# A linear-attention kernel with a squared-relu layer behind it: four paired squares split, and the five engines' lists reordered

## The chip, the cores and the metric

The kernel runs on one core of one Trainium2 chip. The metric is the device time of one execution in microseconds (us). In the profile PE is TensorE (matmuls), PEld its weight loads, DVE VectorE, ACT ScalarE, POOL GpSimd and SP SyncE, which here only issues transfers. L1051 is line 1051 of the kernel's file.

## What is computed

A gated linear attention over 768 tokens for 4 batches of 8 heads with 48 channels, and behind it, token by token, a two-layer network with a squared relu:

```
for t in range(S):
    state = alpha[:, :, t, :, None] * state + einsum('bhd,bhe->bhde', k[:, :, t], v[:, :, t])
    y[:, :, t] = einsum('bhd,bhde->bhe', q[:, :, t], state)
x = y.transpose(0, 2, 1, 3).reshape(3072, 384)
h = x @ w_in              # w_in is 384 x 2048
r = maximum(h, 0.0)
out = (r * r) @ w_out     # w_out is 2048 x 384
```

Inputs and output are float32.

## The kernel before, in words

The 3072 tokens are cut into 12 **units** of 256 tokens: unit g is batch g % 4 and a third g // 4 of its sequence. A unit passes through a fixed series of steps, each of which is one entry in the list of one engine. A step's name is its kind and its unit, so `re5_3` is the relu of group 3 of unit 5. Those that the text speaks of:

- Loads `lda`, `ldk`, `ldq`, `ldv` of the unit's alpha, k, q and v (L540, 384 KB each, on SP or GpSimd), and `win0` to `win2`, `wout0`, `wout1` of the weights (L508, GpSimd). `lda3` and `lda4` wait for `wout0` to have landed.
- Decays: `pr` multiplies the alphas of two neighbouring tokens (L656 on VectorE, L658 on GpSimd), `ln` takes the logarithm (L659), `m1i` and `m1s` form running sums on TensorE (L668), `ei`, `ea`, `es` and `ec` take exponentials on ScalarE (L679, L681, L693, L684), `bk` and `aq` multiply by alpha (L686 or L688, L697), `ekm` and `eqm` scale k and q (L737, L732).
- Attention: `tr` transposes the scaled k and q, in units 0 to 2 on TensorE (copied out by `et`), from unit 3 on by two transfers on SP (L748). `p` forms the scores (L926), `mk` masks them (L937), `vc` casts v (L727, L728), `y` forms the output (L818 to L865), with the next unit's state matmuls `kv` inside it (L797). `sa`, `sc` and `sd` carry the state on. `xe` copies y out of PSUM (L957), `xt` transposes it, from unit 7 on by a transfer on SP (L978), otherwise on TensorE with a copy `xv` (L984).
- First layer: eight groups u of 256 hidden channels, each of six matmuls `s1_g_u` (L1030), a relu `re` out of PSUM (ScalarE L1038 or VectorE L1040) and a square `sq` (VectorE L1048, GpSimd L1051, ScalarE L1052). The groups share two or three PSUM banks, so a group's matmuls wait for the relu of the group before the last. The squares of groups 0 to 5 are made two at a time: `sq5_1` squares groups 0 and 1 of unit 5 in one instruction of 1024 columns. Groups 6 and 7 are squared singly, `sq5_6` and `sq5_7`, 512 columns each.
- Second layer: in units 0, 1, 2 and 11 plain matmuls in quarters, `s2_g_j_q` (L1168), where j says which of two halves of the tokens and quarter q reads groups 2q and 2q+1. Units 3 to 10 use a form with seven products `m1` to `m7` in two halves each (L1096); its operand sums `ga`, `gb`, `gc` (L1080, L1082, L1083) are made on VectorE or GpSimd, `ws` are sums of weights, and `ca` to `cg` collect the products. `oe` copies the plain results out, `out` stores them.
- `fill` steps are matmuls on zeros near the start (L1231) that compute nothing.

The order of the work is **written out by hand**: `ORDERS` holds one list of step names for each engine (ACT, DVE, POOL, SP and PE, L12 on). An engine works its list strictly from front to back. The program derives the waits on semaphores from what each step reads and writes. Moving a name to another list moves the step to that engine. Fractions of work never pass each other within a list: a step that isn't ready holds up all that stand behind it.

The pairing of squares is decided in `first_layer` by the lines

```
if half == 0 and u < nb - 2:
    continue

k = 2 if half == 1 and u < nb - 2 else 1
```

where nb is 8 and half says which of a pair's two relu buffers the group fills.

Of the kernel before, what the change touches and what calls it, by code (L numbers as in the profile page):

```python
# [11 lines left out]
ORDERS = {  # L12
    "act": """
        table ln0_0 ln1_0 #23 ei0_0 ea0_0 ei1_0 ea1_0 et00_0 ec1_0 ec0_0 vc0 et11_0 ln1 ei1 ea1 xe0 xv0 ec1 re0_0
        re0_2 re0_3 xe1 re0_4 re0_5 ln2 sq0_5 ei2 re1_1 ea2 ec2 re1_4 es2 re1_3 re1_5 sq1_1 re1_7 et1_2 sq1_6 sq1_3
        sq1_5 oe0_0 ln3 ei3 ea3 ec3 vc3 es3 ln4 xe2 ei4 ea4 oe0_1 oe1_0 sa3 ec4 lm4 re2_1 es4 re2_2 re2_3 sq2_1 vc4
        re2_5 lm5 lm6 xe3 ln5 re2_7 ei5 ea5 ec5 sq2_5 re3_1 re3_0 re3_3 es5 oe2_0 re3_2 ln6 sq3_3 xe4 ei6 ea6 ec6
        re3_7 sq3_5 es6 sq3_7 re3_6 oe2_1 re4_1 re4_0 sq4_1 lm7 ca3 re4_2 ln7 xe5 ei7 re4_3 ea7 sq4_3 ec7 re4_5 re4_6
        lm8 re4_7 es7 sq4_7 re5_0 re5_1 sq4_5 re5_2 sq4_6 re5_3 ln8 xe6 ei8 re5_5 ea8 re5_4 es8 re5_7 cc4 re5_6 sq5_3
        re6_0 lm9 sq5_5 ln9 re6_1 re6_2 lm10 re6_3 ei9 re6_4 ea9 re6_5 sq6_1 re6_6 re6_7 sq6_3 es9 re7_1 re7_0 cc5  # L20
        sq6_5 re7_3 re7_2 ln10 xe8 sq7_1 ei10 ea10 re7_4 re7_5 ca6 lm11 re7_6 re7_7 es10 re8_0 cc6 re8_1 sq7_7 sq7_5
        re8_2 xe9 ln11 re8_3 ei11 ea11 sq8_1 sq8_3 es11 cc7 re8_6 re8_7 sq8_7 re9_0 sq8_5 sq8_6 xe10 re9_3 sq9_3 re9_5
        sq9_1 cc8 re9_6 sq9_6 sq9_5 re10_1 sq10_1 re10_3 xe11 re10_5 ca9 sq10_3 re10_4 sq10_5 re10_6 re11_0 re11_1
        sq10_6 re11_2 re11_3 sq11_3 ca10 re11_5 cc10 re11_7 sq11_6 oe11_10
    """,
    "dve": """
        #19 #2 #11 #16 #4 #10 #3 #8 #7 #5 #1 #13 #17 #18 #12 #9 #6 ekm0_0 eqm0_0 ekm1_0 et10_0 eqm1_0 et01_0 mk0_0 sa0
        mk1_0 sc0 ekm1 eqm1 et0_1 et1_1 mk1_1 mk0_1 sa1 re0_1 sq0_1 sq0_3 pr2 xv1 re0_7 re0_6 sq0_6 bk2 re1_2 re1_0
        ekm2 aq2 sc1 eqm2 et0_2 ws0_0 re1_6 ws2_0 ws1_1 mk1_2 mk0_2 sa2 sc2 bk3 ekm3 sq1_7 aq3 eqm1_3 eqm0_3 ws2_1 xv2
        sd2 re2_0 ekm4 lb4 sc3 eqm1_4 eqm0_4 mk0_3 mk1_3 re2_4 sa4 oe1_1 sc4 xv3 re2_6 bk5 lb5 ekm5 mk1_4 mk0_4 eqm1_5  # L30
        eqm0_5 sq3_1 sa5 re3_5 sc5 re3_4 lb6 xv4 eqm1_6 ekm6 gb3_0 eqm0_6 mk1_5 mk0_5 pr7 ga3_1 sa6 sc6 ws3_1 re4_4
        cb3 xv5 cc3 ekm7 lb7 cd3 ga4_0 ce3 mk1_6 eqm1_7 eqm0_7 mk0_6 cf3 cg3 gb4_0 ga4_1 sa7 ca4 gb4_1 sc7 xv6 cb4 lb8
        ekm8 eqm0_8 mk1_7 mk0_7 eqm1_8 cd4 ce4 ga5_0 sa8 xe7 cf4 sq5_6 ga5_1 cg4 gb5_1 lb9 eqm1_9 gc5_1 ca5 ekm9 cb5
        mk0_8 eqm0_9 mk1_8 cd5 gc5_0 ga6_0 ce5 sa9 cf5 ga6_1 gb6_1 gc6_0 cg5 sq7_3 lb10 cb6 ekm10 sq7_6 mk0_9 mk1_9
        cd6 eqm0_10 eqm1_10 ga7_0 ce6 sa10 ga7_1 cg6 re8_4 cf6 re8_5 ca7 cb7 lb11 ekm11 eqm0_11 eqm1_11 mk0_10 cd7
        mk1_10 ce7 cf7 re9_1 ga8_1 cg7 re9_2 sa11 ca8 re9_4 mk0_11 re9_7 cb8 mk1_11 re10_0 cd8 ga9_1 ce8 gb9_1 re10_2
# [6 lines left out]
        fill512_15 fill256_16 tr0_1 xt0 tr1_1 fill512_17 fill512_18 fill512_19 fill256_20 p0_1 s1_0_2 s1_0_0 s1_0_1
        kv1 s1_0_3 y1 s1_0_4 s1_0_5 xt1 s1_0_7 s1_0_6 m1i2 s1_1_2 s1_1_1 m1s2 s1_1_0 s1_1_4 s1_1_5 s1_1_3 s1_1_7 tr0_2
        s1_1_6 s2_0_0_0 tr1_2 s2_0_0_1 s2_0_1_0 p0_2 s2_0_1_1 s2_0_0_2 s2_0_0_3 kv2 s2_0_1_2 m1i3 s2_0_1_3 s2_1_0_0
        s2_1_0_1 m1s3 y2 m1i4 s2_1_0_2 xt2 s2_1_0_3 s1_2_0 s1_2_1 s2_1_1_0 s2_1_1_1 s1_2_2 s1_2_3 p0_3 s2_1_1_2 s1_2_5
        s1_2_4 s2_1_1_3 y3 s1_2_6 s1_2_7 xt3 m1i5 s2_2_0_0 s1_3_1 s2_2_0_1 s1_3_0 p0_4 s2_2_0_2 s1_3_3 s2_2_0_3 s1_3_2
        s1_3_5 y4 s2_2_1_0 s1_3_4 m1i6 s1_3_7 xt4 s2_2_1_1 s2_2_1_2 s1_3_6 s2_2_1_3 s1_4_1 p0_5 s1_4_0 s2_3_m10 s1_4_3
        s2_3_m11 s1_4_2 y5 s2_3_m20 s1_4_4 m1i7 s2_3_m60 s2_3_m61 s2_3_m21 xt5 s1_4_6 s2_3_m70 s1_4_5 s2_3_m50
        s2_3_m71 s2_3_m51 s1_4_7 p0_6 s2_3_m40 s1_5_0 s1_5_1 s2_3_m30 s1_5_2 s2_3_m41 s1_5_3 s2_3_m31 y6 s2_4_m10  # L50
        s2_4_m60 s2_4_m11 s1_5_5 m1i8 xt6 s2_4_m61 s1_5_4 s2_4_m20 s2_4_m21 s1_5_7 s1_5_6 p0_7 s2_4_m70 s1_6_1 s1_6_0
        s2_4_m50 s2_4_m71 s2_4_m51 s1_6_2 y7 s2_4_m30 s2_4_m40 s2_4_m41 s1_6_3 m1i9 s1_6_4 s2_4_m31 s2_5_m60 s1_6_5
        s2_5_m10 s2_5_m11 s1_6_6 s1_6_7 s2_5_m61 p0_8 s2_5_m20 s2_5_m21 s1_7_1 s1_7_0 s2_5_m70 s2_5_m71 s1_7_3 s1_7_2
        s2_5_m50 s2_5_m51 s2_5_m40 y8 s2_5_m41 s2_5_m30 s1_7_4 s2_6_m60 m1i10 s2_5_m31 s1_7_5 s2_6_m61 s2_6_m10
        s2_6_m11 s1_7_6 s1_7_7 p0_9 s2_6_m20 s2_6_m70 s1_8_0 s2_6_m21 s2_6_m71 s1_8_1 s1_8_2 s2_6_m50 y9 s2_6_m51
        s2_6_m40 s1_8_3 s2_6_m30 s2_6_m31 s1_8_4 s2_6_m41 s2_7_m10 m1i11 s1_8_5 s2_7_m60 s2_7_m11 s2_7_m61 s1_8_6
        s2_7_m20 s1_8_7 s2_7_m70 s2_7_m21 p0_10 s2_7_m50 s2_7_m51 s2_7_m71 s1_9_0 s1_9_1 s2_7_m40 s2_7_m41 s1_9_2 y10
        s2_7_m30 s2_7_m31 s1_9_3 s2_8_m10 s2_8_m60 s2_8_m11 s1_9_5 s1_9_4 p0_11 s2_8_m20 s1_9_7 s2_8_m61 s2_8_m21
        s1_9_6 s2_8_m50 s1_10_1 s1_10_0 s2_8_m70 s2_8_m51 s2_8_m71 s1_10_2 s1_10_3 s2_8_m40 s2_8_m41 y11 s2_8_m30
        s2_8_m31 s1_10_5 s2_9_m10 s2_9_m11 s1_10_4 s1_10_7 s2_9_m20 s2_9_m60 s2_9_m21 s2_9_m61 s1_10_6 s2_9_m70  # L60
        s2_9_m50 s2_9_m51 s1_11_0 s1_11_1 s2_9_m71 s1_11_2 s1_11_3 s2_9_m40 s2_9_m41 s2_9_m30 s2_9_m31 s1_11_4
        s2_10_m10 s2_10_m11 s2_10_m60 s1_11_5 s2_10_m61 s2_10_m20 s2_10_m21 s2_10_m70 s2_10_m71 s2_10_m50 s1_11_6
# [4 lines left out]
        #14 #20 #15 #21 #22 lda1 ldk1 ldq1 win1 win0 win2 lda2 vc1 ldq2 sd0 ldk2 ldv2 wout0 wout1 vc2 sq0_7 sd1 ldk3
        ldv3 pr3 ws0_1 pr4 bk4 pr6 sq2_3 ws1_0 pr5 ws3_0 sd3 sq2_6 sq2_7 vc5 sd4 ga3_0 bk6 sq3_6 sd5 vc6 gb3_1 bk7 pr8
        gc3_0 gc3_1 vc7 sq5_1 gc4_0 bk8 sq5_7 vc8 gc4_1 pr9 sd6 gb5_0 bk9 pr10 sq6_7 sd7 sq6_6 vc9 gb6_0 bk10 pr11
        vc10 gc6_1 gb7_0 gb7_1 gc7_1 bk11 ga8_0 vc11 gc7_0 gb8_0 gb8_1 gc8_1 gc8_0 sq9_7 gb9_0 sq10_7 gc9_1 gb10_0  # L70
        gb10_1 sq11_1 gc10_1 sq11_5
# [278 lines left out]
def bass_gla_recurrent__then__act_relu_squared_kernel(  # L350
# [658 lines left out]
    def first_layer(g):  # L1009
# [4 lines left out]
        nb = FT // per  # L1014
        for u in range(nb):
            rb, half = h_i[0] // 2 % NRR, h_i[0] % 2
# [23 lines left out]
                alts={"dve": (lambda e, psF=psF, rr=rr: e.tensor_scalar(rr, psF, 0.0, None, ALU.max),  # L1040
                              dve_ns(512))})
# [6 lines left out]
            add("dve", lambda e, dst=dst, sq=sq: e.tensor_tensor(dst, sq, sq, ALU.mult), 148 + k * 267, pu + 1200,  # L1048
# [215 lines left out]
```

## Time and profile before

| what | value |
|---|---|
| time, median of 3 runs | 170.78 us (170.48 to 170.87) |
| profiled execution, its time | 169.46 us |
| profiled execution, its span | 167.7 us |
| busy share of the span | PE 96%, PEld 83%, DVE 79%, ACT 72%, POOL 58% |
| squares on GpSimd | 4 of 1024 columns, 9 of 512 |
| bytes moved | 32.80 MB |

The span is the time from the first to the last thing that the profiler saw; the execution's own time is a little longer. Matmuls overlap one another in the array, so a busy share of PE counts time in which at least one is under way. A row of the timeline gives the start, the duration, the engine, the line, what is written and read, and in brackets the idle time ahead of it with what ended it. The chain of work that ended last is followed back from the end: each piece is what released the next one. A row of a stage gives, for each engine, its busy time and number of instructions, then the granted TensorE clock (1.00 is full), the share of the transfer engines in use and the GB/s moved.

### The profile page before, as it was taken

To read this page: it belongs to the slowest core of one execution; us is meant where nothing else is said; L and a number is where in the kernel's file an instruction comes from. 1 tells how busy PE (TensorE), PEld (TensorE's weight loads), DVE (VectorE), ACT (ScalarE), POOL (GpSimd) and SP (SyncE) were. 2 spreads that over 40 slices of the span, in tenths; PEclk is the share of its full clock that TensorE was granted. 3 is DMA by queue.
4 is the path that set the end of the run, shared out by engine and by line. 5 is a ranking of instruction groups with operands and counts; after the bars stand their busy time and mean duration, and the time that the engine had idled before them with its cause. 6 is when DMAs were issued, how large, how long until landed. Compare 5 with 4: busy or idle time off the path is not lost.

```text
span 167.7 us, 5626 instructions
## 1 busy us (share of the span) xinstructions
PE 160.9 (96%) x2431; PEld 139.6 (83%) x2431; DVE 131.9 (79%) x234; ACT 121.3 (72%) x214; POOL 96.8 (58%) x93
## 2 busy tenths in 40 slices
...
GB/s 135 327 319 209 275 303 216 200 338 267 161 230 166 229 295 124 294 160 263 282 163 327 241 136 336 141 193 334 133 203 139 148 10 4 152 87 94 0 98 94
DMA packets 68232, 32.80 MB, mean 196 GB/s; under 512 B 64144, under 2 KB 65168, under 8 KB 68208
## 3 DMA queue, kind: packets, MB, share of 16 engines
...
## 4 chain that ended last, share of the span: by engine, by line
PE 75%; DMA 15%; POOL 4%; DVE 3%; issue 1%; ACT 1%
PE psWH L1030 32%; PE psO L1096 13%; PE psWH L1096 10%; PE psO L1168 7%; DMA win<-in_moe_w_in_dram 7%; DMA wout<-in_moe_w_out_dram 5%; DMA raw<-in_alpha_dram 3%; PE psX L829 2%; PE psX L926 2%; PE psZ L797 2%; POOL raw L540 2%; PE psX L818 2%; PE psX L998 2%; PE psZ L926 1%; PE psX L972 1%; POOL win L508 1%
## 5 line engine op out<-in xcount | busy, mean ns | idle before, releaser
L1030 PE MATMUL psWH<-xt,win 128*128 128x256 bf16 x552 | 71.7, 273 | 0.2 <-DMA win<-in_moe_w_in_dram 0.2
L1030 PEld LDWEIGHTS psWH<-xt,win 128*128 128x128 bf16 x552 | 60.1, 129 | 2.1 <-DVE xt L984 0.4
L1038 ACT ACTIVATE rr<-psWH 128x512 bf16<-128x512 f32 x70 | 40.9, 595 | 18.3 <-PE psWH L1030 17.2
L1052 ACT ACTIVATE gt<-rr 128x1024 bf16<-128x1024 bf16 (+1 forms) x38 | 35.1, 940 | 2.8 <-PE psWH L1096 1.6
L1051 POOL TENSOR_TENSOR gt<-rr 128x512 bf16<-128x512 bf16 (+1 forms) x13 | 18.6, 1432 | 14.8 <-ACT rr L1038 9.7
L1082 POOL TENSOR_TENSOR gt<-sg,gt 128x512 bf16<-128x512 bf16 x10 | 12.0, 1202 | 12.6 <-DVE sg L1080 12.6
L1040 DVE TENSOR_SCALAR rr<-psWH 128x512 bf16<-128x512 f32 x22 | 15.0, 685 | 5.1 <-PE psWH L1030 5.0
L1168 PE MATMUL psO<-wout,gt 128*128 128x384 bf16 x96 | 18.4, 326 | 0.0
L937 DVE TENSOR_TENSOR pm<-psZ,caus 128x1024 bf16<-128x1024 f32 x12 | 14.6, 1218 | 1.9 <-PE psZ L926 1.9
L937 DVE TENSOR_TENSOR pm<-psX,caus 128x1024 bf16<-128x1024 f32 x12 | 14.6, 1215 | 0.6 <-PE psZ L926 0.5
L1096 PE MATMUL psWH<-sw,gt 128*128 128x192 bf16 x128 | 14.8, 246 | 0.0
L1096 PE MATMUL psO<-wout,gt 128*128 128x192 bf16 x128 | 14.7, 246 | 0.0
L1083 POOL TENSOR_TENSOR sh<-gt 128x512 bf16<-128x512 bf16 x11 | 14.2, 1298 | 0.7 <-DVE gt L1082 0.5
L1168 PEld LDWEIGHTS psO<-wout,gt 128*128 128x128 bf16 x96 | 8.8, 98 | 4.6
L686 POOL TENSOR_TENSOR ek<-ek,raw 128x384 f32<-128x384 f32 x7 | 7.1, 1008 | 9.6 <-ACT ek L679 9.6
L1127 DVE TENSOR_TENSOR osb<-psWH,osb 128x192 f32<-128x192 f32 x24 | 8.4, 350 | 5.0 <-PE psWH L1096 4.9
L737 DVE TENSOR_TENSOR qks<-raw,ek 128x768 bf16<-128x768 f32 x11 | 11.7, 1063 | 0.4 <-ACT ek L644 0.4
L1080 DVE TENSOR_TENSOR sg<-gt 128x1024 bf16<-128x1024 bf16 x14 | 10.6, 754 | 0.9 <-PE psO L1096 0.9
L1096 PEld LDWEIGHTS psWH<-sw,gt 128*128 128x128 bf16 x128 | 10.9, 98 | 0.3
L1096 PEld LDWEIGHTS psO<-wout,gt 128*128 128x128 bf16 x128 | 10.6, 98 | 0.5
L957 ACT ACTIVATE xbf<-psX 128x768 bf16<-128x768 f32 x11 | 8.9, 806 | 2.9 <-PE psX L818 1.7
L732 DVE TENSOR_TENSOR qks<-raw,eq 128x384 bf16<-128x384 f32 x18 | 10.4, 604 | 0.7 <-DMA raw<-in_q_dram 0.7
...
## 6 DMA issues: line engine op xcount, KB each, us to landing
out_dram<-osb SPq DMA_DIRECT2D x11, 384.0 KB, 4.8
raw<-in_alpha_dram SPq DMA_DIRECT2D x10, 384.0 KB, 5.1
raw<-in_q_dram SPq DMA_DIRECT2D x10, 384.0 KB, 5.5
raw<-in_v_dram SPq DMA_DIRECT2D x10, 384.0 KB, 4.8
raw<-in_k_dram SPq DMA_DIRECT2D x9, 384.0 KB, 5.2
...
raw<-in_k_dram POOLq DMA_DIRECT2D x3, 384.0 KB, 6.4
raw<-in_alpha_dram POOLq DMA_DIRECT2D x2, 384.0 KB, 6.0
```

The costliest lines, as they stand in the source:

```text
L737: add("dve", lambda e, a=a, E=E: e.tensor_tensor(QKS[qs][:, a, :, :, 0:D], RAW[r][:, 1 + a].rearrange("p h j d -> p j h d"), E[la][:].rear ...
L937: add("dve", lambda e, hf=hf, psT=psT: e.tensor_tensor(PM[pm][:, hf].rearrange("p r n j t -> p (r n) (j t)"), psT[:, :, :].rearrange("p r ...
L1030: ins = pe.matmul(psF[:, i * T:(i + 1) * T], WIN[:, kk, hidden(fj)], mov, start=(kk == 0), stop=(kk == KT - 1))
L1038: add("act", lambda e, psF=psF, rr=rr: e.activation(rr, psF, AF.Relu), act_ns(512), pu + 600, reads=[keyF], writes=[("rr", rb, half)], nam ...
L1040: alts={"dve": (lambda e, psF=psF, rr=rr: e.tensor_scalar(rr, psF, 0.0, None, ALU.max), dve_ns(512))})
L1051: alts={"pool": (lambda e, dst=dst, sq=sq: e.tensor_tensor(dst, sq, sq, ALU.mult), 200 + k * 840), "act": (lambda e, dst=dst, sq=sq: e.act ...
L1052: "act": (lambda e, dst=dst, sq=sq: e.activation(dst, sq, AF.Square), act_ns(k * 512))})
L1080: ga = lambda e, us=us: e.tensor_tensor(SG[:, us], view(us, 128, [[0, 2], [1, 128]]), view(us, 0, [[384, 2], [1, 128]]), ALU.subtract)
L1082: gb = lambda e, us=us: e.tensor_tensor(G4[:, us, 0, 1], SG[:, us, 1], G4[:, us, 0, 0], ALU.subtract)
L1083: gc = lambda e, us=us: e.tensor_tensor(SH[:, us], G4[:, us, 1, 0], G4[:, us, 0, 1], ALU.add)
L1096: ins = pe.matmul(psS, left(u), right(u), start=(first and u == 0), stop=(u == nu - 1), skip_group_check=True)
L1168: ins = pe.matmul(psS, GT[gt][:, fj, j, :], WOUT[:, fj, :], start=(fj == 0), stop=(fj == FT - 1))
```

## The change

Two things change.

First, a set `ALONE` names four pairs of groups, (2, 3), (5, 1), (11, 1) and (11, 5). In these, each group is squared by an instruction of its own, 512 columns, as groups 6 and 7 always were. So four steps become eight: `sq2_2`, `sq5_0`, `sq11_0` and `sq11_4` are new. All four pairs were squared on GpSimd.

```
+    ALONE = ((2, 3), (5, 1), (11, 1), (11, 5))
...
-            if half == 0 and u < nb - 2:
+            alone = u >= nb - 2 or (g, u | 1) in ALONE
+            if half == 0 and not alone:
                 continue
 
-            k = 2 if half == 1 and u < nb - 2 else 1
+            k = 1 if alone else 2
```

Second, all five lists are written anew. TensorE's holds the same steps in another order, with 16 fillers of 512 columns and 9 of 256 instead of 15 and 6. Between ScalarE, VectorE and GpSimd some 70 steps change their engine. From GpSimd to VectorE go, among others, `pr6`, `pr10`, `pr11`, `sq0_7`, `gb3_1` and `ga3_0`; from VectorE to GpSimd `pr2`, `bk2`, `pr7`, `gb3_0`; from ScalarE to GpSimd six paired squares; and between ScalarE and VectorE 16 steps one way and 20 the other, most of them relus. On SP the steps are the same in another order. The places that the prediction speaks of, before and after:

```
 act, unit 0 to 3
-  re0_0 re0_2 re0_3 xe1 re0_4 re0_5 ln2 sq0_5 ei2 re1_1 ea2 ec2 re1_4 es2 re1_3 re1_5 sq1_1 re1_7 et1_2 sq1_6 sq1_3
-  sq1_5 oe0_0 ln3 ei3 ea3 ec3 vc3 es3 ln4 xe2 ei4
+  re0_0 re0_2 re0_1 xe1 sq0_3 ln2 re0_7 re0_6 es2 re1_1 ei2 re1_0 ea2 re1_4 re1_3 sq1_1 re1_7 re1_5 ec2 et1_2 sq1_3
+  sq1_7 sq1_5 ln3 oe0_0 ei3 ea3 ec3 es3 vc3 oe0_1 ln4 xe2 ei4
 dve, unit 0 to 3
-  sa1 re0_1 sq0_1 sq0_3 pr2 xv1 re0_7 re0_6 sq0_6 bk2 re1_2 re1_0 ekm2 aq2 sc1 eqm2 et0_2 ws0_0 re1_6 ws2_0 ws1_1
-  mk1_2 mk0_2 sa2 sc2 bk3 ekm3 sq1_7 aq3 eqm1_3 eqm0_3 ws2_1 xv2 sd2
+  sa1 sq0_1 re0_3 re0_4 re0_5 xv1 sq0_5 sq0_7 sq0_6 aq2 re1_2 ekm2 sc1 eqm2 ws0_0 re1_6 et0_2 ws2_0 sq1_6 ws1_1
+  mk1_2 mk0_2 sa2 sc2 bk3 ekm3 aq3 eqm0_3 eqm1_3 ws2_1 pr6 xv2 sd2
 pool, from wout0
-  wout0 wout1 vc2 sq0_7 sd1 ldk3 ldv3 pr3 ws0_1 pr4 bk4 pr6 sq2_3 ws1_0 pr5 ws3_0 sd3 sq2_6 sq2_7 vc5 sd4
+  wout0 pr2 wout1 vc2 bk2 sd1 ldk3 ldv3 pr3 ws0_1 pr4 bk4 sq2_2 ws1_0 pr5 sd3 ws3_0 sq2_3 sq2_6 sd4 vc5
 pe, around y2
-  s2_0_0_3 kv2 s2_0_1_2 m1i3 s2_0_1_3 s2_1_0_0 s2_1_0_1 m1s3 y2 m1i4 s2_1_0_2 xt2 s2_1_0_3 s1_2_0
+  s2_0_0_3 kv2 m1i3 s2_0_1_2 s2_1_0_0 m1s3 s2_0_1_3 s2_1_0_1 y2 s2_1_0_2 m1i4 xt2 s2_1_0_3 s1_2_0
 pe, around y11
-  s2_8_m40 s2_8_m41 y11 s2_8_m30 s2_8_m31 s1_10_5 s2_9_m10 s2_9_m11 s1_10_4
+  s2_8_m30 s2_8_m40 s2_8_m31 s1_10_5 s2_9_m10 s2_8_m41 y11 s2_9_m11 s1_10_4
 sp, from xt10
-  xt10 out6_1 xt11 out8_1 out7_1 out9_1
+  xt10 out7_1 out6_1 out8_1 xt11 out10_1 out9_1
 pool, unit 11
-  gb10_0 gb10_1 sq11_1 gc10_1 sq11_5
+  gb10_0 gb10_1 sq11_3 sq11_5 sq11_4 sq11_7
```

107 lines of the change are left out of this document (54 added, 53 removed).

## The prediction

> **What bounds the kernel now.** I read the page's first part, then the busy time by stage, then who waited for whom, then the chain that ended last. The first line says how full each engine is, the second fence which stages leave TensorE idle, and its last line is the only wait of a matmul between 40 and 165.3 us.
>
> ```profile
> PE 160.9 (96%) x2431; PEld 139.6 (83%) x2431; DVE 131.9 (79%) x234; ACT 121.3 (72%) x214; POOL 96.8 (58%) x93
> ```
>
> ```profile
> 35.00:40.00 5.00, 4.05 (x40) 2.06 (x38) 4.51 (x6) 3.56 (x8) 3.50 (x3) 1.00 1.07 313
> 40.00:45.00 5.00, 4.95 (x90) 3.71 (x91) 4.17 (x9) 3.77 (x10) 2.29 (x2) 1.00 1.01 202
> ...
> 130.00:140.00 10.00, 10.00 (x130) 9.64 (x131) 7.24 (x13) 6.96 (x10) 5.76 (x5) 1.00 0.26 67
> ```
>
> ```profile
> PE psX L858 <- DVE qks L737: 0.9, 1, 0.9
> ```
>
> The reader is to see that TensorE (the first pair of each stage) has 0.95 us of idle time from 35 to 40 us and practically none behind it, at a granted clock of 1.00. The one wait is that of y2, the attention output of unit 2. From 40.05 us to the last matmul the time is the sum of TensorE's own instructions; what the other engines do there is hidden as long as it is in time. What sets the start of that stretch is a chain from a load to y2:
>
> ```profile
> 29.32 5.54 DMA raw<-in_alpha_dram
> ...
> 34.94 1.01 POOL prd L658
> ...
> 37.00 0.50 ACT ek L679
> ...
> 37.53 1.39 DVE ek L688
> ...
> 38.95 0.97 DVE qks L737
> ...
> 40.05 0.36 PE psX L858 x8
> ```
>
> Unit 3's alpha lands at 34.87 (29.32 + 5.54); pr3, ln3, m1i3, ei3, bk3 and ekm3 follow, and y2, which holds unit 3's state matmuls, starts 0.13 us after ekm3's end at 39.92.
>
> **The change, part by part.** TensorE's list holds the same work in both kernels, apart from four more fillers (15 of 512 and 6 of 256 columns become 16 and 9) ahead of unit 0's first-layer matmuls, where TensorE waits for loads anyway. What stands ahead of y2 is the same set of steps in both lists, and so is what stands behind it. So a gain behind 40.05 us can't come from TensorE doing less, and a loss comes only from a step that some queue delivers late. I therefore laid the new TensorE list end to end from 40.05 with the durations of the chain's rows, and asked of each moved step whether its engine's new queue delivers in time.
>
> *The halved squares.* The rows by shape:
>
> ```profile
> L1051 POOL TENSOR_TENSOR gt<-rr 128x512 bf16<-128x512 bf16 x9 | 10.9, 1213 | 10.1 <-ACT rr L1038 5.5 <-DVE rr L1040 4.5
> ...
> L1051 POOL TENSOR_TENSOR gt<-rr 128x1024 bf16<-128x1024 bf16 x4 | 7.7, 1925 | 4.7 <-ACT rr L1038 4.2 <-ACT osb L1123 0.5
> ...
> L1052 ACT ACTIVATE gt<-rr 128x512 bf16<-128x512 bf16 x10 | 6.2, 625 | 1.1 <-DVE rr L1040 1.1
> ...
> L1048 DVE TENSOR_TENSOR gt<-rr 128x512 bf16<-128x512 bf16 x5 | 2.1, 416 | 0.0
> ```
>
> Four squares of 1.925 us on GpSimd (7.70 us) become eight of half the size. Six stay there (sq2_2, sq2_3, sq5_0, sq5_1, sq11_4, sq11_5: 6 x 1.213 = 7.28 us), sq11_0 goes to ScalarE (0.625) and sq11_1 to VectorE (0.416). The sum over engines, 8.32 us, is 0.62 more, on engines with 21% to 42% of idle time, so it costs nothing unless a matmul waits for one of them. The square of unit 5 (first row below) was done at 82.84, and the matmuls that read it begin at 97.67; those of unit 11 run from 160.10:
>
> ```profile
> 80.94 1.90 POOL L1051 TENSOR_TENSOR gt<-rr 128x1024 bf16<-128x1024 bf16 x1 [0.92 <-ACT rr L1038]
> ```
>
> ```profile
> 97.67 0.66 PE psO L1096 x8
> ...
> 160.10 2.60 PE psO L1168 x16
> ```
>
> Unit 5 has 14 us to spare. For unit 11, by the same laying out, sq11_7 on GpSimd ends near 160.8 and the quarter that reads it begins at 162.05 (160.10 and three quarters of 2.60). Both cost 0; if that cover of 1.2 us were gone, the excess would be paid in full. Unit 2 is the place that counts.
>
> *Unit 2.* GpSimd, ScalarE, the load queue with its landing (the last number of its row), VectorE and the chain, before:
>
> ```profile
> 48.15 1.90 POOL L1051 TENSOR_TENSOR gt<-rr 128x1024 bf16<-128x1024 bf16 x1 [3.29 <-ACT rr L1038]
> 50.00 1.65 POOL L1060 TENSOR_TENSOR sw<-wout 128x768 bf16<-128x768 bf16 x1
> 51.60 1.02 POOL L658 TENSOR_TENSOR prd<-raw 128x384 f32<-128x384 f32 x1
> 52.58 1.64 POOL L1060 TENSOR_TENSOR sw<-sw,wout 128x768 bf16<-128x768 bf16 x1
> 54.18 0.83 POOL L901 TENSOR_TENSOR sbd<-tmp,acm 128x384 bf16<-128x384 f32 x1
> ```
>
> ```profile
> 46.82 1.25 ACT L1038 ACTIVATE rr<-psWH 128x512 bf16<-128x512 f32 x2
> ```
>
> ```profile
> 46.27 0.60 SPq L540 DMA_DIRECT2D raw<-in_alpha_dram  x1
> ```
>
> ```profile
> raw<-in_alpha_dram SPq DMA_DIRECT2D x1, 384.0 KB, 4.8
> ```
>
> ```profile
> 54.67 0.75 DVE L688 TENSOR_TENSOR ek<-ek,raw 128x384 f32<-128x384 f32 x1
> ```
>
> ```profile
> 55.13 0.65 PE psO L1168 x4
> ```
>
> The last row is s2_2_0_1, which reads what sq2_2 and sq2_3 write. Before, that square was done at 50.05, five us ahead. In the new GpSimd list the first half stands alone early, and the second half comes behind ws1_0, pr5, sd3 and ws3_0. sq2_2 starts when re2_2 ends (46.82 + 0.60 = 47.42) and takes 1.0 to 1.2, to 48.5; ws1_0 takes 1.64, to 50.2. pr5 needs unit 5's alpha, which lands at 46.27 + 4.8 = 51.07. In the new VectorE list sq1_7 (0.42) no longer stands ahead of the steps that release the transposes in front of that load, so it lands between 50.65 and 51.07. Then pr5 1.02, sd3 0.83, ws3_0 1.64 and sq2_3 1.04 make 4.53 us: sq2_3 ends between 55.18 and 55.6 and TensorE wants it at 55.13. That is +0.05 to +0.47. Two bounds lie outside: 0, if the load is early and sq2_3 follows ws1_0's end at 50.2 with no gap (54.7), and +1.1, if bk5 on VectorE (54.67, 0.75) runs first and sq2_3 waits for it. I take **+0.2**, near the early end, where the shorter queue points.
>
> *The start of y2.* pr2 and bk2 go to GpSimd, behind the first and second load of w_out; aq2, two relus and squares are dealt anew. Walking the new lists from 20 to 37 us with the durations above leaves sd1, the loads behind it, pr3 and ln3 where they are; in the new list oe0_0 fits between ln3 and ei3. So bk3 again meets pr4 on GpSimd:
>
> ```profile
> 37.50 0.99 POOL L658 TENSOR_TENSOR prd<-raw 128x384 f32<-128x384 f32 x1
> ```
>
> ```profile
> L688 DVE TENSOR_TENSOR ek<-ek,raw x2: 550/966/1383, 25.2 to 37.5; 128x384 f32<-128x384 f32 x2
> ```
>
> ```profile
> 38.62 0.84 ACT L728 ACTIVATE vbf<-raw 128x768 bf16<-128x768 f32 x1 [0.39 <-DMA raw<-in_v_dram]
> ```
>
> bk3 took 1.383 us where bk2 took 0.550, with pr4 begun 0.03 us before it. If bk3 were first, ekm3 would end 0.83 us sooner. But vc3, the cast of unit 3's values (0.84), now stands behind es3 on ScalarE and ends near 39.95 by my walk, so y2 keeps its start: **0**, bounds -0.1 and +0.15. [...]
>
> *pr6 goes to VectorE*, between ws2_1 and xv2, unit 2's copy to the first layer's input:
>
> ```profile
> 33.50 1.20 SPq L540 DMA_DIRECT2D raw<-in_alpha_dram  x1
> ```
>
> ```profile
> raw<-in_alpha_dram SPq DMA_DIRECT2D x1, 384.0 KB, 7.2
> ```
>
> ```profile
> 41.56 0.55 DVE L1062 TENSOR_TENSOR sw<-wout,sw 128x768 bf16<-128x768 bf16 x1
> 42.72 0.56 DVE L984 COPY xt<-psX 128x768 bf16<-128x768 bf16 x1 [0.60 <-PE psX L972]
> ```
>
> Its load lands at 40.7 and the gap of 0.60 us ahead of xv2 takes a product of 0.55: **0**, bound +0.05. Queued behind it are xv2 and, behind that, TensorE's s1_2_0; a landing later than 42.1 would be paid in full.
>
> *Unit 11's transpose.* y11 moves 1.64 us later in TensorE's list (five half phases), and on SP three stores (out7, out6, out8) now stand ahead of xt11 instead of one:
>
> ```profile
> 142.24 0.77 PE psO L1096 x8
> ...
> 148.59 1.31 PE psWH L1030 x12
> ```
>
> ```profile
> 143.26 1.22 SPq L978 DMA_TRANSPOSE xt<-xbf x1
> ```
>
> ```profile
> DMA to landing us min/median/max: 2.8/2.8/2.8
> ```
>
> ```profile
> DMA to landing us min/median/max: 4.4/4.4/4.4
> ```
>
> y11 ended at 142.24 and the transpose was issued 1.02 us later; the two landing rows are this one and the slowest of its kind, unit 8's. In the new list y11 ends near 144.0, xt11 is issued at 145.0 and lands at 147.8 (2.8) to 149.4 (4.4); s1_11_0 wants it at 149.0. **0**, bound +0.5. The many other swaps between ScalarE, VectorE and GpSimd in units 3 to 10 left margins of 0.2 us or more where I walked them; I take 0 with a bound of +0.3.
>
> **The sum** is 0 + 0.2 + 0 + 0 + 0 = +0.2 us. The profiled execution took 169.46 us (its span of 167.72 and 1.74 around it), so it would become 169.66. The median of the runs shown, 170.78, lies 1.32 above that execution; with the same offset the time is **171.0 us**. A measurement here tells about 0.2%, 0.34 us, from no change.
>
> **The rivals.** *(a) Slower: GpSimd's queue delivers sq2_3 late.* The point from which it decides is unit 5's alpha landing: 55.13 - 4.53 = 50.60 us. Later than that, TensorE stands for the difference, and if bk5 then gets in first, for 0.75 more: +0.47 to +1.1, or 171.3 to 171.9. For it speaks that the load landed at 51.07; against it that its queue is relieved by 0.4. Chance 0.32. *(b) Slower: xt11 lands late* behind out8, issued only 1.5 us ahead of it: +0.5, 171.3, from a landing time over 3.9 us on. The row of 2.8 was taken with no store shortly ahead. Chance 0.06. *(c) Faster: the waits that this one execution doesn't show.* The timed runs were 1.32 us longer; if part of that is TensorE waiting on queues that the new lists relieve (VectorE has fewer relus to do ahead of ekm2), or if y2 starts earlier by the 0.83 of bk3 and vc3 with it, the time falls by 0.4 to 0.8: 170.0 to 170.4. Against it: no row shows such a wait behind 40.05. Chance 0.2. *(d) The change does nothing to the time*, because no matmul waited for the squares: 170.8. It shares its side of the bound with my forecast; both together 0.42.
>
> **How the numbers follow.** Forecast and (d) lie within 0.2%: same 0.42. (a) and (b): slower 0.38. (c): faster 0.20. The range runs from (c)'s middle, 170.1, to (a)'s upper end, 171.9, which also covers the forecast with (b) and the bounds of the small terms; it leaves out the lower half of (c) and sums of several bounds. The likeliest cases alone span 170.5 to 171.1.
>
> **What would show it.** In the profile of the changed kernel: a wait of TensorE for GpSimd's square (L1051) near 55 us, of 0 to 0.5 us, right for unit 2; GpSimd waiting for unit 5's alpha ahead of prd L658 near 50.5; y2 still starting within 0.2 us of 40.05; xt11 landing ahead of s1_11_0; no matmul waiting for squares of units 5 and 11. Wrong would be: y2 starting at 39.2 or behind 40.5, the wait at unit 2 absent or over 1 us, or idle time of TensorE in units 3 to 10, which my walk took for hidden.

## The result, and the profile after

| | before | after |
|---|---|---|
| time, median | 170.63 us (169.30 to 170.87, 4 runs) | 175.40 us (174.57 to 176.12, 4 runs) |
| ratio | | 1.029, 95% interval 1.024 to 1.035 |
| profiled execution, its time and span | 169.46, 167.7 us | 175.80, 174.1 us |

The kernel became slower by 4.8 us, outside the range on record (170.1 to 171.9). Medians in this document are of all runs of a kernel, ratios compare the undisturbed ones alone (one run of e1, two each of e9 and e13), and the profiled executions of e1, e9, e13 and e14, which were disturbed, serve only to see what waits for what.

The two profiled executions lie 6.34 us apart (169.46 and 175.80), 1.6 more than the medians, because before's is near the quickest of its runs and after's lies above its median. The waits in this section are those of after's execution.

The page's first part, the transfer engines' busy share in 40 slices, and the shares of the chain that ended last, of after (line numbers are 1 or 2 higher than before's), and the last of these of before:

```profile
PE 163.0 (94%) x2433; PEld 140.4 (81%) x2435; DVE 137.9 (79%) x234; ACT 119.6 (69%) x214; POOL 104.6 (60%) x97
...
DMA  5999999999896899999999989996796640310042
...
PE 52%; DMA 24%; DVE 9%; SPq 6%; POOL 4%; issue 3%; ACT 2%
```

```profile
PE 75%; DMA 15%; POOL 4%; DVE 3%; issue 1%; ACT 1%
```

TensorE is two points less full, and the chain runs along it less: 52% of it is matmuls, where it was 75%, and 30% is transfers and SP's issuing (DMA and SPq), where DMA was 15%. The transfer engines are 90% busy in most of the slices up to 125 us, so a transfer has neighbours wherever it is put; before, they were as full. The stages, with the same columns as in the prediction:

```profile
35.00:40.00 5.00, 4.18 (x41) 2.08 (x39) 4.75 (x7) 3.29 (x8) 3.59 (x3) 1.00 1.00 289
40.00:45.00 5.00, 4.96 (x90) 3.85 (x90) 4.62 (x9) 3.56 (x9) 1.01 (x1) 1.00 0.90 197
...
60.00:65.00 5.00, 3.51 (x83) 2.82 (x81) 2.67 (x5) 2.85 (x5) 2.72 (x2) 1.00 1.02 297
80.00:90.00 10.00, 8.73 (x171) 7.87 (x170) 7.73 (x14) 7.58 (x15) 6.55 (x7) 1.00 1.09 235
110.00:120.00 10.00, 8.28 (x123) 7.88 (x120) 8.49 (x14) 7.04 (x12) 7.85 (x7) 1.00 1.15 183
```

Up to 45 us nothing has changed. Behind that, stages have holes of 1.3 to 1.7 us. These are the matmuls of after's timeline that stood idle for over 0.2 us (in brackets), from 36 us on:

```profile
36.67 0.34 PE L669 MATMUL psWH<-lab,linc 128*128 128x384 bf16 x1 [0.82 <-ACT lab L660]
...
48.04 0.42 PE L927 MATMUL psX<-kqt 64*64 64x128 bf16 x16 [0.57 <-DVE qks L733]
...
61.24 0.18 PE L819 MATMUL psX<-sbd,kqt 64*128 64x48 bf16 x1 [0.26 <-POOL vbf L728]
...
65.08 0.34 PE L669 MATMUL psZ<-lab,linc 128*128 128x384 bf16 x1 [1.31 <-DVE smd L893]
...
85.54 0.85 PE L1031 MATMUL psWH<-xt,win 128*128 128x256 bf16 x6 [1.27 <-ACT rr L1039]
...
117.52 0.42 PE L927 MATMUL psX<-kqt 64*64 64x128 bf16 x16 [1.72 <-DVE osb L1129]
...
155.06 0.82 PE L1031 MATMUL psWH<-xt,win 128*128 128x256 bf16 x6 [0.38 <-DMA xt<-xbf]
```

The six behind 40 us add up to 0.57 + 0.26 + 1.31 + 1.27 + 1.72 + 0.38 = 5.51 us. The last unit's second layer begins 6.35 us later than before (160.10 then); the 0.84 between is in gaps below 0.2 us, which weren't followed:

```profile
166.45 2.60 PE psO L1170 x16
```

The engine named in brackets is only the last link. The chain of work, followed back from the three long waits, shows what stands behind them:

```profile
55.48 6.84 DMA raw<-in_q_dram
62.34 1.61 DVE qks L733 x2
...
64.56 0.48 DVE smd L893
65.08 0.34 PE psZ L669
...
72.76 1.79 SPq L749
74.58 2.72 SPq L749
...
78.63 4.79 DMA raw<-in_alpha_dram
83.44 0.53 ACT la L702
...
85.00 0.49 ACT rr L1039
85.54 0.85 PE psWH L1031 x6
```

At 65 us it is unit 5's q: issued at 55.48, behind the store out0_1, it took 6.84 us to land, and VectorE, which works its list in order, stood at eqm1_5 and eqm0_5 (L733) with a relu and sa5 (L893) behind them. At 85 us it is unit 8's alpha: lda8 stands behind tr0_6, tr1_6 and ldv7 on SP, is issued at 78.63, and ScalarE, whose next entry is lm8 (L702, the step that reads this alpha), holds two squares and the relu that TensorE needs. Before, lda8 was issued at 68.18, and ldq5 ahead of the store at 55.05 and landed in 4.9:

```profile
55.05 0.63 SPq L540 DMA_DIRECT2D raw<-in_q_dram  x1
55.73 1.51 SPq L1184 DMA_DIRECT2D out_dram<-osb  x1
...
68.18 1.15 SPq L540 DMA_DIRECT2D raw<-in_alpha_dram  x1
```

```profile
raw<-in_q_dram SPq DMA_DIRECT2D x1, 384.0 KB, 4.9
```

At 117 us it is the second transpose of unit 9. SP's list in after, and the landing of its last row:

```profile
103.82 0.58 SPq L1147 DMA_DIRECT2D out_dram<-osb  x1
...
104.92 1.29 SPq L1147 DMA_DIRECT2D out_dram<-osb  x1
106.25 4.09 SPq L749 DMA_TRANSPOSE kqt<-qks  x1
...
111.03 3.38 SPq L749 DMA_TRANSPOSE kqt<-qks  x1
```

```profile
kqt<-qks SPq DMA_TRANSPOSE x1, 6.4
```

111.03 + 6.4 = 117.43, and the scores p0_9 start at 117.52. Before, both transposes were issued in one stretch from 102.81 on. The row of the matmul names VectorE's osb only because a step there ended at the same time (117.08 + 0.34 = 117.42); p0_9 reads the transposed q and k (kqt) and no osb, and the step on VectorE that frees its bank, lb10 (L704), had ended at 115.79. Between the two transposes stands ldq10, and ahead of both two stores and ldq11.

### The profile page after: what moved, and what is told of

Same layout as the page of the kernel before. It is cut to its first block, busy times and chain, and to the rows that moved or that the text cites. A ratio compares the mean times of both kernels' runs of the same rounds, so it can differ in the third digit from the quotient of the medians.

```text
span 174.1 us, 5640 instructions
## 1 busy us (share of the span) xinstructions
PE 163.0 (94%) x2433; PEld 140.4 (81%) x2435; DVE 137.9 (79%) x234; ACT 119.6 (69%) x214; POOL 104.6 (60%) x97
## 4 chain that ended last, share of the span: by engine, by line
PE 52%; DMA 24%; DVE 9%; SPq 6%; POOL 4%; issue 3%; ACT 2%
PE psWH L1031 20%; PE psO L1098 10%; PE psWH L1098 7%; DMA win<-in_moe_w_in_dram 7%; DMA raw<-in_alpha_dram 6%; DMA wout<-in_moe_w_out_dram 5%; SPq L749 4%; DMA raw<-in_q_dram 4%; PE psO L1170 4%; DMA xt<-xbf 3%; DVE pm L938 2%; POOL raw L541 2%; DVE qks L733 2%; PE psX L999 2%; PE psX L927 1%
## 5 line engine op out<-in xcount | busy, mean ns | idle before, releaser
L1039 ACT ACTIVATE rr<-psWH 128x512 bf16<-128x512 f32 x77 | 45.1, 595 | 20.7 <-PE psWH L1031 19.7
L1053 POOL TENSOR_TENSOR gt<-rr 128x512 bf16<-128x512 bf16 (+1 forms) x18 | 23.6, 1315 | 15.5 <-ACT rr L1039 10.9
L1054 ACT ACTIVATE gt<-rr 128x1024 bf16<-128x1024 bf16 (+1 forms) x34 | 30.6, 913 | 0.6 <-DVE rr L1041 0.4
L1170 PE MATMUL psO<-wout,gt 128*128 128x384 bf16 x96 | 18.9, 326 | 0.0
L1084 POOL TENSOR_TENSOR gt<-sg,gt 128x512 bf16<-128x512 bf16 x11 | 14.3, 1308 | 6.7 <-DVE sg L1082 6.6
L733 DVE TENSOR_TENSOR qks<-raw,eq 128x384 bf16<-128x384 f32 x18 | 12.1, 701 | 3.0 <-DMA raw<-in_q_dram 2.3
L738 DVE TENSOR_TENSOR qks<-raw,ek 128x768 bf16<-128x768 f32 x11 | 12.4, 1123 | 0.7 <-ACT ek L645 0.3
L1085 POOL TENSOR_TENSOR sh<-gt 128x512 bf16<-128x512 bf16 x8 | 10.7, 1346 | 3.1 <-DVE gt L1084 3.1
L1041 DVE TENSOR_SCALAR rr<-psWH 128x512 bf16<-128x512 f32 x15 | 10.3, 684 | 2.5 <-PE psWH L1031 2.5
L1170 PEld LDWEIGHTS psO<-wout,gt 128*128 128x128 bf16 x96 | 8.7, 98 | 4.4
L728 POOL CAST vbf<-raw 128x768 bf16<-128x768 f32 x9 | 7.7, 860 | 7.3 <-DMA raw<-in_v_dram 7.3
L958 ACT ACTIVATE xbf<-psX 128x768 bf16<-128x768 f32 x10 | 8.1, 809 | 4.3 <-PE psX L819 2.6
```

The costliest lines, as they stand in the source:

```text
L733: add("dve", lambda e, j=j, dst=dst: e.tensor_tensor(dst, RAW[r][:, 2, :, j, :].rearrange("p (n x) d -> p n x d", x=2), EQ[la][:, j].rearr ...
L738: add("dve", lambda e, a=a, E=E: e.tensor_tensor(QKS[qs][:, a, :, :, 0:D], RAW[r][:, 1 + a].rearrange("p h j d -> p j h d"), E[la][:].rear ...
L1039: add("act", lambda e, psF=psF, rr=rr: e.activation(rr, psF, AF.Relu), act_ns(512), pu + 600, reads=[keyF], writes=[("rr", rb, half)], nam ...
L1053: alts={"pool": (lambda e, dst=dst, sq=sq: e.tensor_tensor(dst, sq, sq, ALU.mult), 200 + k * 840), "act": (lambda e, dst=dst, sq=sq: e.act ...
L1054: "act": (lambda e, dst=dst, sq=sq: e.activation(dst, sq, AF.Square), act_ns(k * 512))})
L1084: gb = lambda e, us=us: e.tensor_tensor(G4[:, us, 0, 1], SG[:, us, 1], G4[:, us, 0, 0], ALU.subtract)
```

## The experiments

Three theories. **S**: the order of SP's list. The new list puts loads and transposes behind stores and behind other loads, they land late, and the engines' strict lists carry the lateness to TensorE. **C**: the new lists of the compute engines. **H**: the halved squares.

### SP's list exchanged, both ways

e1_sp_before is after with before's whole list on SP, e2_sp_after is before with after's whole list on SP; nothing else differs.

```diff
 # e2_sp_after, against before
-"sp": the list of before
+"sp": the list of after
```

> The changed kernel with one list put back: SP issues its loads, transposes and stores in the order of the kernel before; all else is the changed kernel. Theory S (the matmuls wait for transfers that the new SP list issues late: unit 5's q, unit 8's alpha, unit 9's and unit 11's transposes, some 3.7 us of the waits in the trace): 171 to 172.5 us, and the waits of a matmul near 63, 84, 116 and 154 us are gone. Theory C (the new lists of VectorE, ScalarE and GpSimd hold the matmuls up, and the transfers only show it): 174 to 176 us, with waits of a like sum. Theory H (the halved squares cost it): 175 us, no change.

> The kernel before with only SP's list of the changed kernel. Theory S: 173 to 175 us, with VectorE waiting for unit 5's q near 60 us and ScalarE for unit 8's alpha near 80. Theory C and theory H: 170.3 to 171.3 us, as the kernel before.

e2: 175.77 us against 170.46, ratio 1.030 (1.025 to 1.035). SP's list alone, with the old compute lists and no halved square, makes as much as the whole change, a little more than S said. Its long waits are those of after at unit 8's alpha and unit 9's transposes (the second was issued at 111.19 and landed 6.6 us later, at 117.79); the wait for sa5 is 0.44 us here:

```profile
82.76 0.84 PE L1030 MATMUL psWH<-xt,win 128*128 128x256 bf16 x6 [1.93 <-ACT rr L1038]
...
117.88 0.42 PE L926 MATMUL psX<-kqt 64*64 64x128 bf16 x16 [1.55 <-issue]
```

e1 didn't give the gain back cleanly: its four runs lie between 172.2 and 178.3 us, too far apart to tell its time. The waits at 85 and 117 are gone. The one at 65 is not (1.47 us): q5, though ahead of the store, landed 6.6 us after its issue, and its two multiplies took 2.73 us where they had taken 1.41. And a new wait of 3.52 us stands at y6:

```profile
88.36 0.19 PE L819 MATMUL psX<-sbd,kqt 64*128 64x48 bf16 x1 [3.52 <-DVE pm L938]
```

The new VectorE list takes eqm0_7 and eqm1_7 ahead of mk1_6 and mk0_6, so it needs unit 7's q early, and only the new SP list loads it early. Here the new VectorE list leans on the new SP list.

### One part of SP's list at a time, on before

```diff
 # e10_only_a8
-... ldk7 lda8 tr0_6 tr1_6 ldv7 ldq7 ...
+... ldk7 tr0_6 tr1_6 ldv7 lda8 ldq7 ...
 # e11_only_tr9
-... lda11 out3_1 ldk10 tr1_9 tr0_9 xt8 ldv10 ldq10 ldk11 ldq11 out4_1 ...
+... lda11 ldk10 out4_1 ldq11 out3_1 tr1_9 ldq10 tr0_9 xt8 ldv10 ldk11 ...
 # e12_only_q5
-... ldv5 ldq5 out0_1 ldk6 ldq6 tr1_5 ... ldq8 out1_1 ldk8 ...
+... ldv5 out0_1 ldq5 ldk6 ldq6 out1_1 tr1_5 ... ldq8 ldk8 ...
```

> Before with one move on SP's list: lda8 from ahead of tr0_6 to behind ldv7, as after has it. S: lda8 is issued some 8 us later, ACT's lm8 holds ACT's queue, PE waits 1.0 to 1.9 us for a relu near 83 us: 171.5 to 172.4. C: no change, 170.6.

> Before with one group moved on SP's list: out4_1, ldq11 and out3_1 ahead of tr1_9, and ldq10 between tr1_9 and tr0_9, as after has them. S: tr0_9 lands 3 to 5 us later and PE waits 1.5 to 1.7 us for it at p0_9: 172.0 to 172.4. C: no change, 170.6.

> Before with one pair moved on SP's list: ldq5 behind out0_1 and out1_1 ahead of tr1_5, as after has them. S: VectorE's eqm multiplies of unit 5 wait 1.7 us and more for q5, PE 0.4 to 1.3 us near 64: 171.0 to 172.0. C: no change, 170.6.

Before took 171.94 us (median) beside these. e11: 174.09, ratio 1.015 (1.005 to 1.025), more than expected. e12: 172.34, 1.008 (1.004 to 1.013). e10: 172.10, 1.004 (0.999 to 1.009), less than expected and not to be told from no change. The three add up to 2.7%, where the whole list made 3.0%, which fits within their intervals. TensorE in e11, and its stages around the wait:

```profile
115.28 0.42 PE L926 MATMUL psX<-kqt 64*64 64x128 bf16 x16 [3.23 <-DMA kqt<-qks]
```

```profile
110.00:115.00 5.00, 2.05 (x21) 1.81 (x19) 2.95 (x5) 3.03 (x7) 1.79 (x2) 1.00 1.26 167
115.00:120.00 5.00, 4.72 (x60) 4.08 (x61) 2.71 (x4) 0.93 (x2) 1.92 (x2) 0.66 0.69 170
```

Here the trace names the transpose itself. The wait is 3.23 us, and in the five us around its end and behind it the granted clock is 0.66: besides the wait itself, this costs about 0.34 x 5 = 1.7 us of matmul time, an estimate from these rows (four matmuls of L1096 took 0.82 us at 115.89, as long as eight at 109.91). In e12 VectorE waits for q5, and TensorE for sa5 behind it:

```profile
62.37 1.03 DVE L732 TENSOR_TENSOR qks<-raw,eq 128x384 bf16<-128x384 f32 x2 [2.14 <-DMA raw<-in_q_dram]
```

```profile
64.52 0.34 PE L668 MATMUL psZ<-lab,linc 128*128 128x384 bf16 x1 [0.69 <-DVE smd L892]
```

In e10 the load was issued at 74.84 and ScalarE waited for it, but the relus behind it were less late than in after, where SP came to lda8 3.8 us later still:

```profile
79.62 0.53 ACT L701 ACTIVATE la<-raw 128x384 f32<-128x384 f32 x1 [1.39 <-DMA raw<-in_alpha_dram]
```

### Repairs on after's SP list

```diff
 # e5_a8
-... ldk7 tr0_6 tr1_6 ldv7 lda8 ldq8 ...
+... ldk7 lda8 tr0_6 tr1_6 ldv7 ldq8 ...
 # e6_tr9
-... xt7 ldk10 out4_1 ldq11 out3_1 tr1_9 ldq10 tr0_9 xt8 ...
+... xt7 ldk10 tr1_9 tr0_9 out4_1 ldq11 out3_1 ldq10 xt8 ...
 # e7_three: e5, e6 and
-... xt10 out7_1 out6_1 out8_1 xt11 ...
+... xt10 xt11 out7_1 out6_1 out8_1 ...
 # e8_four: e7 and
-... ldv5 out0_1 ldq5 ldk6 ldq6 out1_1 tr1_5 tr0_5 ldv6 ...
+... ldv5 ldq5 out0_1 ldk6 ldq6 tr1_5 tr0_5 ldv6 out1_1 ...
```

> After as it is, with one load moved on SP's list: lda8 from behind ldv7 to ahead of tr0_6. Late transfers (S): ACT's lm8 no longer holds ACT's queue at 83.4 us, the 1.27 us wait of s1_5 for a relu at 85.5 is gone, and the kernel gains 0.8 to 1.3 of its 4.8 us: 174.1 to 174.6; tr0_6 and tr1_6 land a little later, which may give 0.2 back. Compute lists (C): nothing moves, 175.4.

> After as it is, with tr1_9 and tr0_9 moved on SP's list to directly behind ldk10, so that out4_1, ldq11, out3_1 and ldq10 come behind them. S: the 1.72 us wait of p0_9 at 117.5 us is gone, 173.7 to 174.2; if the two transposes still land late among the other transfers, half of it. C: 175.4.

> After with both moves and xt11 ahead of out7_1, out6_1 and out8_1. S: the three waits of 1.27, 1.72 and 0.38 us go, 172.0 to 172.6; what stays is the wait for q5 at 65 us (1.31) and the small ones at 48 and 61 (0.57 and 0.26). C: 175 or more.

> The three moves and, besides, ldq5 ahead of out0_1 as in the kernel before, and out1_1 behind ldv6. S: if the wait at 65 us comes from ldq5's place behind the store, 170.7 to 171.3. If it comes from VectorE's own list (the two relus or q5's multiplies met by GpSimd's order) and not from the load's place, as the run with the list of before on SP hints, where q5 was issued early and landed late all the same, no gain over the three moves: 172.0 to 172.6. C: 175 or more.

S missed in all four: 175.56, 175.39, 182.93 and 182.65 us. C's figures (175.4, and 175 or more) came out in all four, though e2 had shown that the new compute lists aren't needed for the loss; the traces show what undid the repairs. In e5 the wait at 85 is gone, as expected, but the time isn't lower within what its interval tells (ratio to before 1.019 to 1.040). Nor does e5 show that the place of lda8 made that wait: in e6 and in e4 further down lda8 stands where after has it and the wait is gone as well. It was issued there at 76.44 and 77.20, against 78.63 in after, and ScalarE stood for it 0.36 us and not at all. That wait hangs on how late SP has become by then. In e6 the transposes are early and p0_9 waits all the same, 1.96 us, for something else on VectorE:

```profile
114.50 0.36 DVE L1126 COPY osb<-psO 128x192 f32<-128x192 f32 x1 [2.28 <-DMA out_dram<-osb]
```

That is ca6, unit 6's first copy to its output buffer. There are three such buffers, so it needs unit 3's store out3_1 to have landed, and I had moved that store behind the transposes. lb10, which frees the bank that p0_9 writes, stands behind it. In e7 and e8 the same happened on a larger scale: SP stood at xt11, which waits until y11 is copied out, and issued it at 150.32, with out6_1 behind it, and unit 9's copy ca9 needs that buffer:

```profile
155.26 0.36 DVE L1126 COPY osb<-psO 128x192 f32<-128x192 f32 x1 [6.03 <-DMA out_dram<-osb]
```

```profile
155.68 1.46 PE L1098 MATMUL psO<-wout,gt 128*128 128x192 bf16 x8 [4.81 <-DVE osb L1126]
```

```profile
155.00:160.00 5.00, 4.32 (x24) 3.73 (x25) 3.28 (x7) 0.00 (x0) 0.00 (x0) 0.50 0.16 59
```

With 4.81 us of wait and a clock of 0.50 around its end and behind it e7 takes 182.93 us, where after took 175.40. One thing in e8 did work: with ldq5 ahead of the store the wait at 65 is gone (1.64 us in e7).

So the next list keeps the two stores ahead that a buffer waits for:

```diff
 # e9_mended: after's SP list with
+... ldv5 ldq5 out0_1 ldk6 ldq6 tr1_5 tr0_5 ldv6 out1_1 lda7 ldq7 ldk7 lda8 tr0_6 ...
+... xt7 ldk10 out3_1 tr1_9 tr0_9 ldq10 ldq11 out4_1 xt8 ldv10 ...
+... xt10 out7_1 out6_1 xt11 out8_1 ...
 # e15_mended2: e9 with
+... xt7 ldk10 out3_1 tr1_9 tr0_9 xt8 ldv10 ldq10 ldk11 ldq11 out4_1 ...
 # e13_sp_before_q7: after with before's SP list and in it
-... lda7 ldk7 lda8 tr0_6 tr1_6 ldv7 ldq7 ldq8 ...
+... lda7 ldq7 ldk7 lda8 tr0_6 tr1_6 ldv7 ldq8 ...
```

> After with its compute lists and the halves, and SP's list mended place by place, now with an eye to who waits for each store: ldq5 ahead of out0_1 and out1_1 behind ldv6; lda8 ahead of tr0_6; out3_1 (whose buffer unit 6's copy needs) still ahead of tr1_9 and tr0_9, and ldq10, ldq11 and out4_1 behind them; xt11 between out6_1 (whose buffer unit 9's copy needs) and out8_1. S with the buffers counted: no wait over 0.6 us from 48 to 155 us but the one that the run with four moves kept at 93 (1.16): 171.2 to 172.5. If the loss is in the compute lists (C) or nothing but disturbance of the transfers that comes back wherever a load is moved: 174 or more.

> The mended list of SP once more, with xt8 and ldv10 directly behind tr0_9 and ahead of ldq10, ldk11, ldq11 and out4_1, where before has them. S: also the wait for v10 at 124 (0.68) gone; 171.0 to 172.5, the same as the run beside it within 0.5%. C: 174 or more.

> After's compute lists and halves with before's list on SP, in which one load is moved: ldq7 ahead of ldk7, as after has it, because VectorE's new list takes unit 7's two multiplies by the decay ahead of mk1_6 and mk0_6. S: the wait of 3.5 us at 88 that the run with the whole list of before showed is gone; 171.0 to 172.5, and what is left of the loss is the compute lists' own, at most 1%. C: 174 or more.

> After itself, unchanged, beside the two mended lists on the same chip. Every theory: 174.6 to 176.1; S has both mended lists 2.5 to 4.5 us below it, C has them level with it.

| | median | ratio to before, interval |
|---|---|---|
| e9_mended | 175.89 us | 1.015 (1.002 to 1.028) |
| e15_mended2 | 173.00 us | 1.014 (1.007 to 1.021) |
| e13_sp_before_q7 | 173.51 us | 1.003 (0.993 to 1.013) |
| e14_after (after itself, beside e13 and e15) | 176.87 us | 1.031 (1.025 to 1.038) |

e15 against e14, whose intervals don't meet, is the test in the other direction: seven entries in other places on SP's list (ldq5, out1_1, lda8, ldq11, ldq10, out4_1, xt11) give back 1.7 of the 3.1%. By the medians e15 lies 3.9 us below e14, as S said (2.5 to 4.5), but 173.00 is above S's 171.0 to 172.5 and below C's 174; e13's median lies between the two as well, e9's met C's figure, and e14 itself came out above its range. What is left of TensorE's waits from 40 to 140 us in e15 is short; three of the five (the others are 0.34 and 0.23):

```profile
55.72 0.82 PE L1170 MATMUL psO<-wout,gt 128*128 128x384 bf16 x4 [0.22 <-POOL gt L1053]
...
74.20 0.32 PE L669 MATMUL psZ<-lab,linc 128*128 128x384 bf16 x1 [0.63 <-ACT lab L660]
...
86.80 0.34 PE L669 MATMUL psZ<-lab,linc 128*128 128x384 bf16 x1 [0.47 <-DVE smd L893]
```

e13 has all of after's compute lists and halves, so its ratio says that they cost at most 1.3% beside that SP list. But it rests on two runs, its interval is wide, and the median of its five, 173.51, isn't below e15's; the wait at 88 that e1 had is gone from it, and one of 1.79 us stands at 95. No list tried here beats before. The first row of e15's waits is GpSimd's square ahead of unit 2's second layer, the place that the prediction had priced.

### The halved squares alone, and taken away

```diff
 # e3_alone: before's five lists, POOL's with the four new halves
-... sq2_3 ... sq5_1 ... sq11_1 ... sq11_5
+... sq2_2 sq2_3 ... sq5_0 sq5_1 ... sq11_0 sq11_1 ... sq11_4 sq11_5
 # e4_pairs: after without the halves (their four new steps out of the lists)
-ALONE = ((2, 3), (5, 1), (11, 1), (11, 5))
+ALONE = ()
```

> The kernel before with only the four pairs of squares halved: each new half stands right ahead of its partner in GpSimd's list, nothing else moves. Theory S and theory C: 170.3 to 171.2 us, since GpSimd has 58% of work and no matmul waits for these squares. Theory H: over 172 us.

> The changed kernel with the four pairs squared together again, at the place of the second half; all lists else as changed. Theory S and theory C: 174.5 to 176 us. Theory H: under 173 us.

e4: 174.84 us, ratio 1.025 (1.020 to 1.030): without the halves after isn't told from after with them (1.024 to 1.035), so H, which said under 173, is out. In e4's execution the wait at 117 is gone with the same order on SP: p0_9, which reads unit 9's transposes, began at 115.19 without a wait, where it began at 117.52 in after. So the split of the loss over the single waits is that of one execution. e3: 171.71, ratio 1.010 (1.004 to 1.017), so not nothing, and above what S and C said (171.2). Its profiled execution, of 169.81 us, is only 0.35 longer than before's and shows one place behind y2, unit 5:

```profile
80.15 2.37 POOL L1053 TENSOR_TENSOR gt<-rr 128x512 bf16<-128x512 bf16 x2 [0.27 <-ACT rr L1039]
```

```profile
79.54 2.08 DVE L733 TENSOR_TENSOR qks<-raw,eq 128x384 bf16<-128x384 f32 x2
```

```profile
82.81 0.19 PE L819 MATMUL psX<-sbd,kqt 64*128 64x48 bf16 x1 [0.41 <-DVE pm L938]
```

The pair had to wait for both relus and began at 80.94. The half begins at 80.15, in the middle of VectorE's two eqm multiplies, which took 1.03 us before and take 2.08 now; the mask behind them, and y6, come later. Why they take twice as long beside the square isn't shown. How much of the 1% this is stays open: 0.41 us is 0.24%.

## Why the prediction was wrong, step by step

- **The failing step** is the one that priced "the many other swaps between ScalarE, VectorE and GpSimd in units 3 to 10" at 0 with a bound of +0.3. It names three engines, and it was the fourth queue that mattered. I had read SP's list for unit 2 and for unit 11 only. In after's execution the waits behind three late transfers, q5, unit 8's alpha and unit 9's second transpose, are 4.3 of the 5.5 us (1.31 + 1.27 + 1.72). That SP's list alone is enough is shown by e2 (+3.0%), two of its parts singly by e11 and e12, and a part of the way back by e15. How much each single entry costs isn't shown: e10 found nothing for lda8, and e4 and e6 lack one or two of the three waits. The sign that the prediction had named for this, idle time of TensorE in units 3 to 10, is what came.
- "A loss comes only from a step that some queue delivers late" was right; that no row showed such a wait behind 40.05 was taken for slack. It was no slack: VectorE already waited 0.46 us for q5 in before, too little to reach TensorE:

```profile
59.97 1.41 DVE L732 TENSOR_TENSOR qks<-raw,eq 128x384 bf16<-128x384 f32 x2 [0.46 <-DMA raw<-in_q_dram]
```

- **Unit 2**, +0.2: not seen, though its parts came out nearly as worked out. GpSimd waited for unit 5's alpha and began pr5 at 50.68, beside the deciding point of 50.60; sq2_3 ended at 54.05 + 1.04 = 55.09 and TensorE read it at 55.57. In the same view, the timeline, it had read it at 54.97 before: the prediction's 55.13 is where the chain's piece begins, 0.16 later than the first of these matmuls. The wait of 0.57 at 48 had put TensorE later, so the square was in time; at 54.97 TensorE would have stood 0.12 for it, and in e15 it does stand 0.22. That sq2_3 would stand for bk5, as the bound of +1.1 and the 0.75 in rival (a) have it, is shown by no run: in after bk5 began at 55.27, behind sq2_3's end, and the longest wait of TensorE for a square of unit 2 in any run is 0.29 us (e4). What the traces show in its place are steps on GpSimd that took longer when they began inside one on VectorE: before, the square begun at 54.97 inside bk5 (54.67, 0.75 us) took 1.36 us where one at 88.83 took 1.04, and in after sd4, begun at 56.68 inside ekm5 (56.21, 1.33 us), took 1.54 where sd3 took 0.83 at 51.65. The rows of pr5 and sq2_3:

```profile
50.68 1.01 POOL L659 TENSOR_TENSOR prd<-raw 128x384 f32<-128x384 f32 x1 [0.29 <-DMA raw<-in_alpha_dram]
...
54.05 1.04 POOL L1053 TENSOR_TENSOR gt<-rr 128x512 bf16<-128x512 bf16 x1
```

- **The start of y2**, 0: right, 40.08 after 40.05. Its wait moved to m1i3 (0.82 at 36.67), which stands ahead of it in the new list. That ekm3 would end 0.83 us sooner with bk3 first, which rival (c) counts on, didn't come out: bk3 came first (37.65) and took 0.56 us, but ekm3, with pr4 beside it from 38.12 on, took 1.69 where it had taken 0.96, and ended at 39.93, as before (39.91).
- **pr6 to VectorE**, 0: no wait of TensorE near 42. **Unit 11's transpose**, 0 with +0.5: 4.4 us of landing and 0.38 of wait, inside the bound, as rival (b) had it, but its mechanism, a store shortly ahead, isn't shown: in e13, with before's one store between xt10 and xt11, TensorE waited 0.26 us for this landing too. What lengthened it is not shown. **The halved squares**, 0: no cost that e4 can tell within after; 1.0% where they are put alone on before's lists, of which the 0.41 us that the trace shows, behind the two multiplies of 2.08 us beside GpSimd's square, is 0.24%. The step didn't look for that.
- Rival (a) had the right sign and the wrong queue, so its sign is no credit to it; for (c), no kernel's ratio lies below 1. The middle of (c)'s 170.0 to 170.4 is 170.2, not 170.1, on which nothing hangs; and the intervals here are half a per cent and more to each side, not 0.2%. What stays open is the 1.4% that e15 keeps: compute lists, halves, or SP's order still. e13 points to SP's order, on two runs.
